# The first chunk's loads and masks put back, and the last store of the last chunk halved, in an mLSTM cell with a GELU feed-forward block

## The chip, the cores and the metric

The kernel runs on one core of a Trainium2 chip. The core has a matrix engine (TensorE, PE in the profile; PEld is its loading of weights), VectorE (DVE), ScalarE (ACT), GpSimd (POOL), and SyncE (SP), which here only issues transfers (DMA). The engines run beside each other, each through its own instructions in order, and wait for each other by semaphores. The metric is the time of one execution on the device, in microseconds.

## The reference

There are 4 batches of 8 heads, a sequence of 768 steps and a head size of 40. An mLSTM cell runs over the sequence, and its output goes through two matrix products with a GELU between them:

```python
for t in range(S):
    m_new = np.maximum(f_gate[:, :, t] + m, i_gate[:, :, t])
    f_stab = np.exp(f_gate[:, :, t] + m - m_new)
    i_stab = np.exp(i_gate[:, :, t] - m_new)
    m = m_new
    C = f_stab[..., None, None] * C + i_stab[..., None, None] * np.einsum('bhd,bhe->bhde', vt, kt)
    n = f_stab[..., None] * n + i_stab[..., None] * kt
    h_tilde = np.einsum('bhde,bhe->bhd', C, qt)
    denom = np.maximum(np.abs(np.einsum('bhd,bhd->bh', n, qt)[:, :, None]), 1.0)
    y[:, :, t] = sigmoid(o_gate[:, :, t]) * h_tilde / denom
x = y.transpose(0, 2, 1, 3).reshape(B * S, H * D)     # 3072 x 320
h = x @ w_in                                          # 320 x 2048
out = (h * sigmoid(1.702 * h)) @ w_out                # 2048 x 320
```

## The kernel before

The sequence is cut into six chunks of 128 steps. In a chunk the recurrence is written as a masked product: scores (queries times keys) are multiplied by weights exp(...) that come from running sums and maxima of the gates, and the product is multiplied by the values. The first chunk has no earlier state. Its weights are built on TensorE from the gates, split in three bf16 parts (`m3`, `a3`). The loads of the first chunk, the conversion of the feed-forward weights and the first chunk's attention all happen at the start; from the second chunk on, a chunk's attention runs beside the feed-forward products of the chunk before.

The parts that the change touches, with cuts marked:

```python
def load_gates(w):
    for dst, src in ((f_sb, f_gate), (i_sb, i_gate)):
        dst[w] = ld.tile([BH, L], FP, tag="fi", bufs=4, name="fi")
        (nc.sync if w > 1 else nc.scalar).dma_start(
            out=dst[w], in_=src[:, :, w * L:(w + 1) * L].rearrange("b h s -> (b h) s"))
# ... cut ...
load_gates(0)
load_gates(1)
for what, n in (("kq", 0), ("kq", 1), ("vo", 0), ("vo", 1), ("kq", 2), (fetch, 0), ("kq", 3),
                (fetch, 1), ("vo", 2), ("vo", 3), *((fetch, n) for n in range(2, 10))):
    ...        # "kq", n: keys and queries of batch n; "vo": values and output gate; fetch: a weight piece
# ... cut ...
keep_busy(7, ps_m, "m")                # filler products on TensorE
# ... cut ...
def clear(t):
    A.copy(out=t, in_=idle[:, 0:1].to_broadcast(t.shape))
# ... cut ...
def gates(w):                          # running sum and maximum on VectorE
    V.tensor_tensor_scan(out=f_run, data0=ones, data1=f_sb[w], ...)            # L258
    V.tensor_tensor(out=a, in0=i_sb[w], in1=f_run, op=OP.subtract)             # L260
    if w == 0:
        V.tensor_tensor(out=neg, in0=f_run, in1=i_sb[w], op=OP.subtract)
        in_three(G, a3, neg, neg, part)                                        # GpSimd
    V.tensor_tensor_scan(out=m_run, data0=ones, data1=a, initial=m, ...)       # L266
    if w == 0:
        in_three(V, m3, m_run, left, part)                                     # VectorE
    ...
# ... cut ...
def causal(x, n):
    G.affine_select(out=x, in_=x, compare_op=OP.is_ge, fill=0.0, base=0, pattern=[[0, n], [1, L]],
                    channel_multiplier=-1)                                     # L325

def weights(w, b):
    if w == 0:
        for i in range(2):
            pw = ps_a.tile([L, NP, L], FP, tag="a", name="p_w")
            if b > 1:                                                          # mask as a product, L334
                T.matmul(pw, ident_bf, not_yet.unsqueeze(1).to_broadcast([L, NP, L]), start=True, stop=False)
            for p in range(NP):
                T.matmul(pw[:, p, :], one, m3, start=(b < 2), stop=False)
                T.matmul(pw[:, p, :], a3, one, start=False, stop=(b < 2 or p == NP - 1))
            A.activation(out=x[:, :, i, :], in_=pw, func=AF.Exp)               # L340
            if b < 2:
                causal(x[:, :, i, :], NP)
        return
    ...
def scores(w, b):
    ...                                                                        # TensorE, L361
    for i in range(2):
        V.tensor_tensor(out=wt[w, b][:, :, i, :], in0=pw[i], in1=wt[w, b][:, :, i, :], op=OP.mult)   # L363
# ... cut: the order of the first chunk ...
transposes(0, 0)
transposes(0, 1, slice(0, 1))          # keys of batch 1
weights(0, 0)
transposes(0, 1, slice(1, 2))          # queries of batch 1
gates(1)
scores(0, 0)
weights(0, 1)
scores(0, 1)
gate_out(0)
gate_out(1)
clear(k_bl.rearrange("p j g c -> p (j g c)"))
values(0, 0)                           # TensorE, L373
values(0, 1)
transposes(0, 2)
convert(0, "A")                        # a weight piece: the part on ScalarE ("A"), on VectorE ("V")
weights(0, 2)
# ... cut ...
clear(state.rearrange("p j a b -> p (j a b)"))
# ... cut ...
convert(2, "V", slice(0, 256))
convert(3)
convert(4)
convert(2, "V", slice(256, 512))
```

At the other end, the second feed-forward product of a chunk is made in seven half-sized products for each pair of batches. Each goes by an addition on VectorE (L631) into the halves of two output tiles, which are then stored:

```python
def store(two):
    b = 2 * c + two
    nc.sync.dma_start(out=out[b * S + w * L:b * S + (w + 1) * L, :], in_=o[two])

return [lambda: product(block(0, 0), w00, (o00, None), (o01, None)),
        lambda: product(block(0, 1), w10, (o00, o00)),          # o00 is final here
        lambda: product(summed(1), t2, (o01, o01)),
        lambda: product(block(1, 0), w01, (o10, o01)),
        lambda: product(summed(0), t1, (o11, o10), (o01, o01)),
        lambda: (product(block(1, 1), t4, (o10, o10)), store(1)),
        lambda: (product(summed(2), w11, (o01, o01)), store(0))]
```

Of the kernel before, what the change touches and what calls it, by code (L numbers as in the profile page):

```python
# [12 lines left out]
OP = mybir.AluOpType  # L13
# [9 lines left out]
L = 128  # L23
# [11 lines left out]
def kernel(  # L35
# [12 lines left out]
    nc = tc.nc  # L48
    B, H, S, D = q.shape
    BH = B * H  # L50
    DM = H * D
    DFF = moe_w_in.shape[1]
    NW = S // L
    NP = H // 2
# [5 lines left out]
    DH = DM // 2  # L60
# [10 lines left out]
    ps_m = ctx.enter_context(tc.tile_pool(name="ps_m", bufs=2, space=PSUM))  # L71
# [3 lines left out]
    V, A, G, T = nc.vector, nc.scalar, nc.gpsimd, nc.tensor  # L75
# [6 lines left out]
    q_bl, k_bl = (const.tile([128, BH // 2, L // 32, 32], FP, name=name) for name in ("q_bl", "k_bl"))  # L82
# [11 lines left out]
    def load_gates(w):  # L94
        for dst, src in ((f_sb, f_gate), (i_sb, i_gate)):
            dst[w] = ld.tile([BH, L], FP, tag="fi", bufs=4, name="fi")
            (nc.sync if w > 1 else nc.scalar).dma_start(
                out=dst[w], in_=src[:, :, w * L:(w + 1) * L].rearrange("b h s -> (b h) s"))

    def load(w, what, bs=slice(0, B)):  # L100
        hs = slice(bs.start * H, bs.stop * H)
# [48 lines left out]
    pieces = []  # L150
# [4 lines left out]
    bits = {}  # L155
# [12 lines left out]


    load_gates(0)  # L170
    load_gates(1)
    for what, n in (("kq", 0), ("kq", 1), ("vo", 0), ("vo", 1), ("kq", 2), (fetch, 0), ("kq", 3),
                    (fetch, 1), ("vo", 2), ("vo", 3), *((fetch, n) for n in range(2, 10))):
        if isinstance(what, str):
            load(0, what, slice(n, n + 1))
        else:
            what(n)
# [5 lines left out]
    not_yet, ident_bf = (xs.bitcast(BF)[:, i * L:(i + 1) * L] for i in range(2))  # L183
# [3 lines left out]
    def keep_busy(n, pool=ps_a, tag="a"):  # L187
        p_idle = pool.tile([128, W], FP, tag=tag, name="p_idle")
        for _ in range(n):
            T.matmul(p_idle, idle, idle.unsqueeze(1).to_broadcast([128, 4, 128]), start=True, stop=True)  # L190

    keep_busy(7, ps_m, "m")
    ident = const.tile([128, 128], FP, name="ident")
    make_identity(nc, ident)
    one1 = const.tile([BH, 1], FP, name="one1")
# [9 lines left out]
    for t in (k_st, q_st):  # L205
# [3 lines left out]
                    channel_multiplier=-1)  # L209
    V.tensor_copy(out=ident_bf, in_=ident)  # L210

    a3 = const.tile([3 * BH, L], BF, name="a3")
    m3 = const.tile([3 * BH, L], BF, name="m3")
    state = const.tile([128, BH // 2, 2, D1], FP, name="state")

    def clear(t):
        A.copy(out=t, in_=idle[:, 0:1].to_broadcast(t.shape))


    t1, t2, t4 = (const.tile([128, NH, DH], FP, name=f"t{i}") for i in (1, 2, 4))  # L220

# [1 line left out]
    cols, stacked, m_row, dec = {}, {}, {}, {}  # L223
    kT, qT, wt, ys, xT, gs, o_ps, p_c = {}, {}, {}, {}, {}, {}, {}, {}


    def convert(n, engines="AV", part=slice(0, 512)):

        lo, hi, dst = bits[n][:, part, 0], bits[n][:, part, 1], pieces[n][0][:, part]
        dst_u = dst.bitcast(U32)  # L230
        if "A" in engines:
            A.activation(out=dst, in_=hi.bitcast(FP), func=AF.Abs)
            A.activation(out=lo, in_=lo, func=AF.Copy, scale=2.0 ** -29)
        if "V" not in engines:
            return
        V.tensor_scalar(out=dst, in0=dst, scalar1=HI_MIN, scalar2=HI_MAX, op0=OP.max, op1=OP.min)
        V.tensor_scalar(out=dst_u, in0=dst_u, scalar1=3, scalar2=0x3FFFFFFF, op0=OP.logical_shift_left,
                        op1=OP.bitwise_and)
        V.scalar_tensor_tensor(out=dst_u, in0=hi, scalar=0xC0000000, in1=dst_u, op0=OP.bitwise_and,
                               op1=OP.bitwise_or)  # L240
        V.tensor_tensor(out=dst_u, in0=dst_u, in1=lo, op=OP.add)
# [59 lines left out]
    def transposes(w, b, which=slice(0, 2)):  # L301
        for bl, st, dst, name in ((k_bl, k_st, kT, "kT"), (q_bl, q_st, qT, "qT"))[which]:
            dst[w, b] = work.tile([128, NP, L], FP, tag=name, bufs=4, name=name)
            if w:
                V.transpose(out=dst[w, b].rearrange("p j t -> p (j t)"),
                            in_=bl[:, b * NP:(b + 1) * NP].rearrange("p j g c -> p (j g c)"))
                continue
            pt = ps_a.tile([128, NP, L], FP, tag="a", name="p_t")
            for p in range(NP):
                h = b * H + 2 * p  # L310
                T.transpose(pt[:, p, :], st[:, h:h + 2, :].rearrange("p a b -> p (a b)"), ident)
            if b == 0:
                keep_busy(1)
            A.copy(out=dst[w, b], in_=pt)
# [5 lines left out]
            nc.sync.dma_start(out=x.rearrange("s p i t -> s (p i) t"),  # L320
                              in_=m_row[w][b * H:(b + 1) * H, :].unsqueeze(0).to_broadcast([L, H, L]))

    def causal(x, n):

        G.affine_select(out=x, in_=x, compare_op=OP.is_ge, fill=0.0, base=0, pattern=[[0, n], [1, L]],  # L325
                        channel_multiplier=-1)

    def weights(w, b):
        if w == 0:
            x = wt[w, b] = work.tile([L, NP, 2, L], FP, tag="wt", bufs=4, name="wt")  # L330
            for i in range(2):
                pw = ps_a.tile([L, NP, L], FP, tag="a", name="p_w")
                if b > 1:
                    T.matmul(pw, ident_bf, not_yet.unsqueeze(1).to_broadcast([L, NP, L]), start=True, stop=False)  # L334
                for p in range(NP):
                    h = b * H + 2 * p + i
                    one = pick[:, h:h + 1].to_broadcast([3 * BH, L])
                    T.matmul(pw[:, p, :], one, m3, start=(b < 2), stop=False)
                    T.matmul(pw[:, p, :], a3, one, start=False, stop=(b < 2 or p == NP - 1))
                A.activation(out=x[:, :, i, :], in_=pw, func=AF.Exp)  # L340
                if b < 2:
                    causal(x[:, :, i, :], NP)
            return
        x = wt[w, b].rearrange("s p i t -> s (p i) t")
        for h in range(H):
            A.activation(out=x[:, h, :], in_=x[:, h, :], func=AF.Exp, scale=-1.0,  # L346
                         bias=cols[w][:, b * H + h:b * H + h + 1])
        causal(x, H)
        if w > 1 and b == 0:
            gates_out(w)  # L350

    def gates_out(w):
        A.activation(out=eo[w], in_=eo[w], func=AF.Tanh, scale=0.5)
# [238 lines left out]
    w10, w11 = w_out_sb[:, NH:NF, 0:DH], w_out_sb[:, NH:NF, DH:DM]  # L592
# [16 lines left out]
    def total(i, c):  # L609

        return (xs if i == 0 and c else big[:, i, :]).rearrange("p (f t) -> p f t", t=L)

    def down_fast(w, c):
        o = [op.tile([128, DM], FP, tag="o", name="o_sb") for _ in range(2)]
        o00, o01, o10, o11 = (o[i][:, n * DH:(n + 1) * DH] for i in range(2) for n in range(2))

        def block(two, k):
            return lambda f: gs[w, k * 4 + f // 2][:, f % 2, (2 * c + two) * L:(2 * c + two + 1) * L]

        def summed(i):  # L620
            return lambda f: total(i, c)[:, f, :]

        def product(a, b, *adds):
            po = ps_m.tile([128, DH], FP, tag="m", name="p_out")
            for f in range(NH):
                T.matmul(po, a(f), b[:, f, :], start=(f == 0), stop=(f == NH - 1))  # L626
            for dst, x in adds:
                if x is None:
                    V.tensor_copy(out=dst, in_=po)
                else:  # L630
                    V.tensor_tensor(out=dst, in0=x, in1=po, op=OP.add)  # L631

        def store(two):
            b = 2 * c + two
            nc.sync.dma_start(out=out[b * S + w * L:b * S + (w + 1) * L, :], in_=o[two])

        return [lambda: product(block(0, 0), w00, (o00, None), (o01, None)),
                lambda: product(block(0, 1), w10, (o00, o00)),
                lambda: product(summed(1), t2, (o01, o01)),
                lambda: product(block(1, 0), w01, (o10, o01)),  # L640
                lambda: product(summed(0), t1, (o11, o10), (o01, o01)),
                lambda: (product(block(1, 1), t4, (o10, o10)), store(1)),
                lambda: (product(summed(2), w11, (o01, o01)), store(0))]

# [24 lines left out]
    def gate_out(b):  # L671
        z = eo[0][:, b * H:(b + 1) * H, :]
        A.activation(out=z, in_=z, func=AF.Tanh, scale=0.5)
# [11 lines left out]
    V.tensor_reduce(out=pair, in_=ident[0:BH, 0:BH].rearrange("p (j two) -> p j two", two=2), axis=AX.X, op=OP.add)  # L685
    V.tensor_copy(out=half[0:BH], in_=par.unsqueeze(2).to_broadcast([BH, 2, 64]))
    transposes(0, 0)
    transposes(0, 1, slice(0, 1))
    weights(0, 0)
    transposes(0, 1, slice(1, 2))  # L690
    gates(1)
    scores(0, 0)
    weights(0, 1)
    scores(0, 1)
    gate_out(0)
    gate_out(1)
    clear(k_bl.rearrange("p j g c -> p (j g c)"))
    values(0, 0)
    values(0, 1)
    transposes(0, 2)  # L700
# [11 lines left out]
    columns(0)  # L712
    gate_out(2)
    gate_out(3)
    clear(state.rearrange("p j a b -> p (j a b)"))
    scale(0, 0)
    scale(0, 1)

# [16 lines left out]
    full_rows(0, 1, 0)  # L735
    seam(0, 3)
    full_rows(1, 1, 0)

    convert(2, "V", slice(0, 256))
    convert(3)  # L740
    convert(4)
    convert(2, "V", slice(256, 512))
    for j in range(2):
        for c in range(2):
            full_rows(j, c, 1)
# [132 lines left out]
```

## Time and profile before

| what | value |
|---|---|
| time, median of 3 runs | 489.21 us (487.54 to 490.1) |
| span of the profiled execution | 485.8 us |
| instructions | 10430 |
| DMA moved | 44.87 MB, 175953 packets, mean 92 GB/s |

The page gives each engine's busy time and its share of the span, then the span in 40 slices of about 12.1 us, one digit for each (tenths, 9 is 90% or more), for the engines and for the DMA engines. A line of an answer on the timeline has the start and duration in us, the engine, the line of the kernel, the operation, what it writes and reads with its shape, and in brackets how long the engine stood idle before it and what ended that. An answer on waits has the total, the number of times and the longest, in us. A group in the timeline can hold several instructions (x16): its duration is from the first start to the last end.

### The profile page before, as it was taken

How to read it: one execution, taken by the hardware profiler on the slowest of the kernel's cores; microseconds unless marked ns; L12 is line 12 of the kernel's file. 1: busy time of each engine (PE TensorE's matmuls, PEld its weight loads, DVE VectorE, ACT ScalarE, POOL GpSimd, SP SyncE). 2: the span in 40 equal slices, each digit the busy share in tenths (PEclk: the TensorE clock that was granted, in tenths of full speed). 3: DMA queues.
4: the chain of work that ended last, by engine and by line, in shares of the span. 5: the costliest groups of instructions: out<-in, count | busy, mean ns of one | idle time of the engine just before them, and what ended most of it. 6: DMA issues, size and time to landing. Idle time of an engine off the chain costs nothing. (4 is left out here: it accounts for less than half of the span.)

```text
span 485.8 us, 10430 instructions
## 1 busy us (share of the span) xinstructions
PE 477.8 (98%) x4067; PEld 396.8 (82%) x4067; DVE 343.7 (71%) x857; ACT 220.2 (45%) x575; POOL 62.6 (13%) x105
## 2 busy tenths in 40 slices
PE   8899999999999999999999999999999999999997
PEld 5784457777879999788999877999977999977997
DVE  7889879787978965667766686696576786254831
ACT  3776768203559401467700465900374920255300
POOL 4120003420000430000331000232000120000000
PEclk9999999999999999999999999999999999999999
DMA  9999789823996100997000796300393000000000
GB/s 135 207 274 325 164 154 245 91 41 69 154 214 69 19 28 29 164 201 80 7 29 2 120 252 74 32 28 3 78 258 29 2 15 16 28 1 0 1 27 28
DMA packets 175953, 44.87 MB, mean 92 GB/s; under 512 B 164352, under 2 KB 169504, under 8 KB 175904
## 3 DMA queue, kind: packets, MB, share of 16 engines
q1 hardware_dynamic: 175136, 43.48, 48.6%
q8 instruction: 32, 0.52, 0.5%
q10 hardware_dynamic: 768, 0.72, 0.4%
q14 instruction: 17, 0.14, 0.1%
HBM read 40.17 MB, written 4.01 MB: 91 GB/s over the span
## 5 line engine op out<-in xcount | busy, mean ns | idle before, releaser
L626 PE MATMUL p_out<-w_out_sb,g 128*128 128x160 f32 x480 | 69.8, 301 | 0.0
L416 ACT COPY xT<-p_x 128x384 f32<-128x384 f32 x24 | 10.8, 482 | 127.5 <-PE p_x L415 114.4
L626 PEld LDWEIGHTS p_out<-w_out_sb,g 128*128 128x128 f32 x480 | 66.3, 190 | 0.9
L537 DVE TENSOR_TENSOR g<-p_u,g 128x256 f32<-128x256 f32 x80 | 33.7, 424 | 44.6 <-PE p_u L529 35.0
L534 ACT COPY g<-p_u 128x256 f32<-128x256 f32 x120 | 43.0, 377 | 43.5 <-PE p_u L529 39.3
L541 ACT ACTIVATE g<-g 128x256 f32<-128x256 f32 x120 | 42.3, 423 | 39.4 <-DVE g L537 39.4
L325 POOL TENSOR_SCALAR_AFFINE_SELECT wt<-wt 128x1024 f32<-128x1024 f32 (+1 forms) x24 | 25.2, 1054 | 236.3 <-ACT wt L346 187.1
L631 DVE TENSOR_TENSOR o_sb<-o_sb,p_out 128x160 f32<-128x160 f32 x70 | 21.4, 317 | 42.2 <-PE p_out L626 41.8
L346 ACT ACTIVATE wt<-wt,cols 128x128 f32<-128x128 f32 x160 | 47.9, 394 | 0.0
L529 PE MATMUL p_u<-xT,w_in_sb 128*128 128x256 f32 x160 | 38.9, 382 | 0.0
L529 PE MATMUL p_u<-xs,big 128*128 128x256 f32 x160 | 37.9, 379 | 0.0
L557 PE MATMUL p_u<-xT,w_in_x 64*128 64x512 f32 x80 | 37.0, 602 | 0.0
L557 PE MATMUL p_v<-xT,w_in_x 64*128 64x512 f32 x80 | 37.0, 602 | 0.0
L577 PE MATMUL p_out<-w_out_sb,g 128*128 128x320 f32 x128 | 36.3, 436 | 0.0
L363 DVE TENSOR_TENSOR wt<-p_s,wt 128x512 f32<-128x512 f32 x48 | 30.4, 682 | 8.1 <-POOL wt L325 6.7
L626 PE MATMUL p_out<-t,big 128*128 128x160 f32 x240 | 35.5, 301 | 0.0
L529 PEld LDWEIGHTS p_u<-xT,w_in_sb 128*128 128x128 f32 x160 | 29.6, 190 | 5.4 <-DVE o_sb L631 1.5
L529 PEld LDWEIGHTS p_u<-xs,big 128*128 128x128 f32 x160 | 30.0, 190 | 4.6
L626 PEld LDWEIGHTS p_out<-t,big 128*128 128x128 f32 x240 | 33.3, 190 | 0.2
L577 PEld LDWEIGHTS p_out<-w_out_sb,g 128*128 128x128 f32 x128 | 23.8, 190 | 9.8 <-issue 0.5
L537 DVE TENSOR_TENSOR g<-p_v,g 128x256 f32<-128x256 f32 x80 | 29.8, 414 | 0.0
L361 PE MATMUL p_s<-qT,kT 40*128 40x128 f32 x384 | 25.7, 280 | 1.9 <-DVE wt L363 1.6
(172 smaller groups left out, 844.8 us busy)
## 6 DMA issues: line engine op xcount, KB each, us to landing
wt<-m_row SPq DMA_DIRECT2D x20, 512.0 KB, 6.6
v_st<-in_v_dram SPq DMA_DIRECT2D x5, 640.0 KB, 9.0
eo<-in_o_gate_dram SPq DMA_DIRECT2D x5, 640.0 KB, 6.0
k_st<-in_k_dram SPq DMA_DIRECT2D x5, 640.0 KB, 11.0
out_dram<-o_sb SPq DMA_DIRECT2D x20, 160.0 KB, 1.8
big<-in_moe_w_in_dram SPq DMA_DIRECT2D x5, 512.0 KB, 7.4
k_bl<-in_k_dram SPq DMA_DIRECT2D x40, 64.0 KB, 2.9
q_bl<-in_q_dram SPq DMA_DIRECT2D x40, 64.0 KB, 2.8
```

Of the source, the lines that this page charges most:

```text
L325: G.affine_select(out=x, in_=x, compare_op=OP.is_ge, fill=0.0, base=0, pattern=[[0, n], [1, L]], channel_multiplier=-1)
L346: A.activation(out=x[:, h, :], in_=x[:, h, :], func=AF.Exp, scale=-1.0, bias=cols[w][:, b * H + h:b * H + h + 1])
L361: T.matmul(pw[i][:, p, :], kT[w, b][r, p, :], qT[w, b][r, p, :], start=True, stop=True)
L363: V.tensor_tensor(out=wt[w, b][:, :, i, :], in0=pw[i], in1=wt[w, b][:, :, i, :], op=OP.mult)
L529: T.matmul(p[k][:, ts[t]], a[:, k // 2, k % 2 * 128:(k % 2 + 1) * 128], b, start=first, stop=True, skip_group_check=True)
L534: A.copy(out=g[k][i][:, ts[t]], in_=chain[k][:, ts[0]])
L537: V.tensor_tensor(out=g[k][i][:, ts[t]], in0=p[k][:, ts[pt]], in1=g[k][i][:, ts[t]], op=OP.add)
L541: A.activation(out=dst, in_=dst if src is None else src, func=AF.Gelu_apprx_sigmoid)
L557: T.matmul(p[k], w_in_x[r, k, :], x[r, 2, :], start=False, stop=True, skip_group_check=True)
L577: T.matmul(po, gs[w, f // 2][:, f % 2, b * L:(b + 1) * L], w_out_sb[:, f, :], start=(f == 0), stop=(f == NF - 1))
L626: T.matmul(po, a(f), b[:, f, :], start=(f == 0), stop=(f == NH - 1))
L631: V.tensor_tensor(out=dst, in0=x, in1=po, op=OP.add)
```

## The change

The change takes back a set of edits to the first chunk, and adds one edit to the last chunk. In the first chunk all gate loads are issued by SyncE again, those of the second chunk behind the keys and queries of batches 0 and 1; the causal mask of batches 0 and 1 is again a product on TensorE and not a select on GpSimd; the keys of batch 1 are transposed with its queries; the two clears stand at the top of ScalarE's program; piece 2 is converted in one go; and there is one more filler product. In the last chunk the left half of batch 2's output rows, which is final after the second product of seven, is stored at once, so that the last store of the kernel has 160 columns and not 320.

```diff
-            (nc.sync if w > 1 else nc.scalar).dma_start(
-                out=dst[w], in_=src[:, :, w * L:(w + 1) * L].rearrange("b h s -> (b h) s"))
+            nc.sync.dma_start(out=dst[w], in_=src[:, :, w * L:(w + 1) * L].rearrange("b h s -> (b h) s"))
 load_gates(0)
-load_gates(1)
-for what, n in (("kq", 0), ("kq", 1), ("vo", 0), ...
+for what, n in (("kq", 0), ("kq", 1), (load_gates, 1), ("vo", 0), ...
-    keep_busy(7, ps_m, "m")
+    keep_busy(8, ps_m, "m")
-    def clear(t):
+    for t in (k_bl.rearrange("p j g c -> p (j g c)"), state.rearrange("p j a b -> p (j a b)")):
         A.copy(out=t, in_=idle[:, 0:1].to_broadcast(t.shape))
# ... cut: weights(0, b) ...
-                if b > 1:
-                    T.matmul(pw, ident_bf, not_yet..., start=True, stop=False)
+                T.matmul(pw, ident_bf, not_yet..., start=True, stop=False)
-                    T.matmul(pw[:, p, :], one, m3, start=(b < 2), stop=False)
-                    T.matmul(pw[:, p, :], a3, one, start=False, stop=(b < 2 or p == NP - 1))
+                    T.matmul(pw[:, p, :], one, m3, start=False, stop=False)
+                    T.matmul(pw[:, p, :], a3, one, start=False, stop=(p == NP - 1))
-                if b < 2:
-                    causal(x[:, :, i, :], NP)
# ... cut: down_fast ...
+        last = w == NW - 1 and c == 1
-        def store(two):
+        def store(two, cols=slice(0, DM)):
             b = 2 * c + two
-            nc.sync.dma_start(out=out[b * S + w * L:b * S + (w + 1) * L, :], in_=o[two])
+            nc.sync.dma_start(out=out[b * S + w * L:b * S + (w + 1) * L, cols], in_=o[two][:, cols])
+        def left_done():
+            if last:
+                store(0, slice(0, DH))
-                lambda: product(block(0, 1), w10, (o00, o00)),
+                lambda: (product(block(0, 1), w10, (o00, o00)), left_done()),
-                lambda: (product(summed(2), w11, (o01, o01)), store(0))]
+                lambda: (product(summed(2), w11, (o01, o01)), store(0, slice(DH if last else 0, DM)))]
# ... cut: the order of the first chunk ...
-    transposes(0, 1, slice(0, 1))
     weights(0, 0)
-    transposes(0, 1, slice(1, 2))
+    transposes(0, 1)
-    clear(k_bl.rearrange("p j g c -> p (j g c)"))
-    clear(state.rearrange("p j a b -> p (j a b)"))
-    convert(2, "V", slice(0, 256))
+    convert(2, "V")
     convert(3)
     convert(4)
-    convert(2, "V", slice(256, 512))
```

More of the change, by code (lines that the diff above doesn't have):

```diff
@@ L170 @@
     load_gates(0)
-    load_gates(1)
-    for what, n in (("kq", 0), ("kq", 1), ("vo", 0), ("vo", 1), ("kq", 2), (fetch, 0), ("kq", 3),
+    for what, n in (("kq", 0), ("kq", 1), (load_gates, 1), ("vo", 0), ("vo", 1), ("kq", 2), (fetch, 0), ("kq", 3),
                     (fetch, 1), ("vo", 2), ("vo", 3), *((fetch, n) for n in range(2, 10))):
@@ L224, with convert @@
     kT, qT, wt, ys, xT, gs, o_ps, p_c = {}, {}, {}, {}, {}, {}, {}, {}
-    def convert(n, engines="AV", part=slice(0, 512)):
-        lo, hi, dst = bits[n][:, part, 0], bits[n][:, part, 1], pieces[n][0][:, part]
+    def convert(n, engines="AV"):
+        lo, hi, dst = bits[n][:, :, 0], bits[n][:, :, 1], pieces[n][0]
         dst_u = dst.bitcast(U32)
@@ L321, in spread @@
                               in_=m_row[w][b * H:(b + 1) * H, :].unsqueeze(0).to_broadcast([L, H, L]))
-    def causal(x, n):
-        G.affine_select(out=x, in_=x, compare_op=OP.is_ge, fill=0.0, base=0, pattern=[[0, n], [1, L]],
-                        channel_multiplier=-1)
     def weights(w, b):
@@ L332, in weights @@
                 pw = ps_a.tile([L, NP, L], FP, tag="a", name="p_w")
-                if b > 1:
-                    T.matmul(pw, ident_bf, not_yet.unsqueeze(1).to_broadcast([L, NP, L]), start=True, stop=False)
+                T.matmul(pw, ident_bf, not_yet.unsqueeze(1).to_broadcast([L, NP, L]), start=True, stop=False)
                 for p in range(NP):
@@ L347, in weights @@
                          bias=cols[w][:, b * H + h:b * H + h + 1])
-        causal(x, H)
+        G.affine_select(out=x, in_=x, compare_op=OP.is_ge, fill=0.0, base=0, pattern=[[0, H], [1, L]],
+                        channel_multiplier=-1)
         if w > 1 and b == 0:
```

## The prediction

> **What bounds the kernel now.** I read the page first: the busy shares, the 40 slices and the chain that ended last. Then I asked for TensorE's waits over the whole span, because the page shows it as the only nearly full engine, and then for the timeline of the first 31 us and of the last 10 us, which are the two places that the change touches. Last came the landings of the first loads, one by one.
>
> ```profile
> span 485.8 us, 10430 instructions
> ...
> PE 477.8 (98%) x4067; PEld 396.8 (82%) x4067; DVE 343.7 (71%) x857; ACT 220.2 (45%) x575; POOL 62.6 (13%) x105
> ...
> PE   8899999999999999999999999999999999999997
> ...
> DMA  9999789823996100997000796300393000000000
> ```
>
> TensorE (PE) is busy for 477.8 of 485.8 us. All that the two ends of the kernel can give or take is within the 8.0 us left: the first two slices (8, 8) and the last (7). Everything between is TensorE in its own order. The DMA row says that the first 75 us or so are also full of transfers, so a load that starts later is a suspect there. TensorE's waits, over the whole span:
>
> ```profile
> PE p_s L361 <- DVE wt L363: 1.6, 1, 1.6
> PE p_idle L190 <- DVE idle L184: 1.1, 1, 1.1
> PE p_w L338 <- DVE m L251: 0.9, 1, 0.9
> PE p_out L626 <- DVE o_sb L631: 0.4, 1, 0.4
> PE p_s L361 <- ACT wt L340: 0.4, 1, 0.4
> PE p_t L311 <- DMA k_st<-in_k_dram: 0.3, 1, 0.3
> ```
>
> Six waits of 0.3 us or more in the whole kernel (one of 0.2 is left out), all but one before 21 us, so the start must be read as a chain. The lines of the timeline that carry it (start, duration, engine; in brackets the idle time before it and what ended it):
>
> ```profile
> 3.58 0.41 DVE L258 TENSOR_TENSOR_SCAN f_run<-one,fi 32x128 f32<-32x128 f32 x1
> 5.67 0.28 DVE L260 TENSOR_TENSOR st<-fi,f_run 32x128 f32<-32x128 f32 x1 [1.68 <-DMA fi<-in_i_gate_dram]
> 8.60 0.23 PE L338 MATMUL p_w<-m,pick 96*128 96x128 bf16 x1 [0.86 <-DVE m L251]
> 9.91 0.41 DVE L258 TENSOR_TENSOR_SCAN f_run<-one,fi 32x128 f32<-32x128 f32 x1
> 10.20 1.27 POOL L325 TENSOR_SCALAR_AFFINE_SELECT wt<-wt 128x512 f32<-128x512 f32 x2 [1.40 <-ACT wt L340]
> 10.35 0.62 DVE L260 TENSOR_TENSOR st<-fi,f_run 32x128 f32<-32x128 f32 x1
> 12.70 0.62 DVE L285 TENSOR_SCALAR dec_in<-pair,both 32x16 f32<-32x16 f32 x1
> 13.24 1.27 DVE L363 TENSOR_TENSOR wt<-p_s,wt 128x512 f32<-128x512 f32 x2
> 13.97 1.16 PE L361 MATMUL p_s<-qT,kT 40*128 40x128 f32 x16 [1.56 <-DVE wt L363]
> 15.23 1.29 DVE L363 TENSOR_TENSOR wt<-p_s,wt 128x512 f32<-128x512 f32 x2 [0.72 <-PE p_s L361]
> 16.57 1.02 PE L373 MATMUL p_o<-v_st,wt 128*64 128x41 f32 x28 [0.24 <-DVE wt L363]
> ```
>
> The reader is to see one chain: the input gate lands (5.67), the first chunk's gates are computed and split in three (to 8.6), the first weights follow (exponential, mask on POOL to 11.47), and then VectorE, which computes the second chunk's gates from 9.91 on, comes to its first product of scores and weights only at 13.24, although the scores were finished at 11.41 (the L361 group of 10.25, 1.16 us). TensorE waits 1.56 us for that product. From 16.57 on it has one wait of 0.36 us left until the end of the first part, so whatever the start gains or loses by 16.57 should stand at the end of the kernel.
>
> At the other end the last addition and the last two stores:
>
> ```profile
> 481.04 2.51 SPq L635 DMA_DIRECT2D out_dram<-o_sb  x2
> 482.86 0.32 DVE L631 TENSOR_TENSOR o_sb<-o_sb,p_out 128x160 f32<-128x160 f32 x1 [1.85 <-PE p_out L626]
> ```
>
> The addition ends at 483.18, the last store is issued then and lands 1.8 us after its issue (about 485.0), and the span closes at 485.8.
>
> [...] the first input-gate load, 16 KB issued by ScalarE at 1.29, took 4.3 us to land, between key loads of 160 KB that took 3.4 to 5.0. The second issuer did not make it a fast load.
>
> [...] L260, two SBUF inputs, takes 0.28 us at 5.67, and 0.62 at 10.35 under POOL's select of 10.20 to 11.47; the scan L266 takes 0.47 alone and 0.73 there; L285 takes 0.62 under the second pair of selects.
>
> [...] This trace has 1.8 us for the whole store of 160 KB[...]; the 16 KB stores of m_row took 1.4 us in the median, which gives (1.8 - 1.4) x 80/144 = 0.22 us for halving the size.
>
> **The change part by part.**
>
> 1. Two gate loads move ahead of the first keys on SyncE's queue. An issue of a gate load there takes 0.42 us (median of the later ones), with the gap about 0.48; two of them put the first keys' issue from 0.81 to about 1.8, so everything behind them lands about 1.0 us later: first keys 4.2 to 5.2, first queries 5.5 to 6.5, second keys 6.9 to 7.9, second queries 7.9 to 8.9. The first gates gain: with nothing ahead of it but the forget gate, the input gate should land after about 2.7 us, as the first forget gate did (0.80, needed at 3.58), so at about 4.1 instead of 5.6. The scans then run 1.5 us earlier: the split in three ends on VectorE at about 7.0 and on POOL at 7.2, instead of 8.55 and 8.81.
>
> 2. The first weights then wait for TensorE's own order, not for the gates: first-query transposes from 6.5, some 0.9 us at the still slow rate, and the filler after them to about 7.7. Start of the weights: 7.7 against 8.60, a gain of 0.9.
>
> 3. Mask on TensorE in place of POOL for batches 0 and 1. Added: four matmuls L334 of 0.38 us. In the third batch, which has them already, matmuls begin 0.22 us after the mask's, so I count 0.22 x 2 = 0.44 us for a batch. Removed: the POOL selects, four of 0.65 us (two in 1.27), of which the end past the exponentials counts: 11.47 - 10.56 = 0.91 us. So batch 0's weights are complete at 7.7 + 1.5 (two groups of 0.75) + 0.7 (the last exponential) = 9.9, instead of 11.47.
>
> 4. Second keys' transposes go behind the weights. That adds 0.63 us of TensorE ahead of the first scores. Both second transposes then run 9.2 to 10.4, and the scores 10.4 to 11.55: the same time as before (11.41), within 0.2.
>
> 5. The second gates. Their loads are now issued seventh and eighth on SyncE's queue, at about 4.6 and 5.1, behind the second queries; small, they should land right behind them, at 9.0 to 9.5 (before: 5.9 and 6.65). VectorE reaches them at about 8.3, and waits. Its work there took 13.24 - 9.91 = 3.33 us before; without POOL beside it (0.62 to 0.28, 0.73 to 0.47, 0.62 to about 0.17) it is 1.05 less, so 2.3 us: 9.2 + 2.3 = 11.5. The first product thus starts at about 11.6 and not at 13.24: 1.6 us earlier.
>
> 6. From there batch 1: weights with masks on TensorE 11.55 to 13.05, scores to 14.2, product at 14.25 against 15.23. TensorE's second half of the values starts about 15.6 against 16.57. Gain carried into the dense part: about 1.0 us.
>
> 7. The clears (1.90 and 1.28 us on ScalarE, at 13.69 and 27.24) move to the first 5.5 us, where ScalarE does nothing until the first keys' copy at about 6.3: no cost, and no gain on TensorE, which didn't wait for ScalarE there.
>
> 8. The second half of weight piece 2's conversion is put ahead of pieces 3 and 4: 0.78 us more (half of 0.43+0.43+0.69+0.69, less overlaps, from L236 to L241 at 30.57 to 32.2). VectorE stood idle 0.87 us just before piece 3 (L236 at 33.07), which takes it up: 0. One more filler matmul, 0.43 us, lies in the wait for the first keys: 0.
>
> 9. The last store is half as large, and the left half is stored some 10 us earlier, beside TensorE's work: -0.2 us. VectorE's later additions go to the other half, and I see no wait of theirs on that store.
>
> Sum: -1.0 (start) - 0.2 (end) = -1.2 us at face value.
>
> **The rivals.** First, the loads' delay comes through. Everything on SyncE's queue is about 1.0 us later, and if the second gates land later than 9.5 (the backlog ahead of them is 640 KB), each us of that is a us of the first product: at 11 they would land for a product at 13.3 and the start would gain nothing. For it: in later chunks gate loads behind a backlog took up to 11.4 us. Against: only four loads are ahead of them. The time would be 489.
>
> Second, later loads take the place of the removed waits. Piece 1 lands at 20.1 and ScalarE takes it at 22.01; both move towards each other by 1.0 us, and 0.1 is missing. The last output gate lands at 24.6, needed 27.0; piece 2 lands at 26.9, taken at 28.42 behind a clear of 1.28 that goes away. These have slack of nil to 1 us. If they bind, the start loses some of its gain but hardly goes below nothing: 488.5 to 489.5.
>
> Third, the parts removed were worth what they were made for: first keys 1.0 us earlier, and second keys transposed in a hole of TensorE. Then the kernel is 1 us slower in the start and 0.2 faster at the end: 490. For it: TensorE's first transposes did wait for keys, and there will be some 0.5 us more of that. The clock adds a doubt: [...] The trace agrees with a switch (the filler L190 took 0.63 us early, 0.38 at 6.48), and a hole of 0.5 us between 4.7 and 5.2 may put it off.
>
> **Range and chances.** I weigh my own chain at a little over half, and the two rivals that eat it at the rest: 0.55 x (-1.2) + 0.3 x (-0.2) + 0.15 x (+0.8) = -0.6, so 489.2 - 0.6 = 488.6 us. Three runs of the kernel before span 2.6 us by themselves (487.54 to 490.1); with 1 us of doubt on the change, a range of 486.8 to 490.4. Two per cent are 9.8 us, more than all of TensorE's idle time (8.0), so faster by that much can't follow from these parts; slower by it would need a jam of the loads that I don't see: 0.01 and 0.02.
>
> **What would show it.** Right: the first VectorE product of scores and weights near 11.6, the second half of batch 1's values on TensorE near 15.6, VectorE's second L260-like subtraction near 0.28 us, first keys' transposes near 5.2, no POOL select before 20 us, TensorE without new waits from 20 to 75 us, and a last store of about 1.6 us. Wrong: a wait of VectorE for the second gates' loads past 10; TensorE idle for a DMA or for a converted piece between 20 and 45 us; or a later addition waiting for the early store.

## The result, and the profile after

The changed kernel takes 485.88 us in the median of 6 runs (485.65 to 486.87). The kernel before, run beside it, takes 489.5 (487.54 to 490.88). The ratio is 0.993, with a 95% interval of 0.9907 to 0.9952. I had forecast 488.6 and a range of 486.8 to 490.4: the time lies outside that range, and the gain of 3.6 us is six times the forecast 0.6.

The page of the changed kernel (PEclk is the clock that TensorE was granted, in tenths of its full speed):

```profile
span 485.1 us, 10434 instructions
...
PE 479.3 (99%) x4072; PEld 397.8 (82%) x4072; DVE 343.0 (71%) x853; ACT 220.6 (45%) x575; POOL 60.4 (12%) x101
...
PE   8999999999999999999999999999999999999997
...
PEclk9999999999999999999999999999999999999999
```

The span of this execution is 485.1 us, only 0.7 below the 485.8 of the one profiled before. That is the first thing to notice: the two profiles differ by much less than the medians. The execution profiled before (487.54) was the fastest of its six, the one profiled after (486.87) the slowest. TensorE's waits:

```profile
PE p_idle L188 <- DVE idle L182: 1.1, 1, 1.1
PE p_out L615 <- DVE o_sb L620: 0.4, 1, 0.4
PE p_o L362 <- DVE wt L352: 0.4, 1, 0.4
PE p_s L350 <- ACT wt L330: 0.4, 1, 0.4
PE p_t L307 <- DMA k_st<-in_k_dram: 0.3, 1, 0.3
```

The wait of 1.6 us for VectorE's first product and the 0.9 for the first gates are gone. The start, in the lines of the timeline that answer to those of before (scan, subtraction, weights, second gates, products):

```profile
3.85 0.28 DVE L256 TENSOR_TENSOR st<-fi,f_run 32x128 f32<-32x128 f32 x1
4.99 1.09 PE L307 MATMUL p_t<-ident,k_st 128*128 128x128 f32 x4 [0.34 <-DMA k_st<-in_k_dram]
7.27 0.38 PE L324 MATMUL p_w<-xs 128*128 128x512 bf16 x1
8.64 0.41 DVE L254 TENSOR_TENSOR_SCAN f_run<-one,fi 32x128 f32<-32x128 f32 x1 [0.49 <-DMA fi<-in_f_gate_dram]
9.09 0.28 DVE L256 TENSOR_TENSOR st<-fi,f_run 32x128 f32<-32x128 f32 x1
10.84 0.22 DVE L281 TENSOR_SCALAR dec_in<-pair,both 32x16 f32<-32x16 f32 x1
10.98 1.27 DVE L352 TENSOR_TENSOR wt<-p_s,wt 128x512 f32<-128x512 f32 x2
12.11 1.35 PE L350 MATMUL p_s<-qT,kT 40*128 40x128 f32 x16
13.37 1.29 DVE L352 TENSOR_TENSOR wt<-p_s,wt 128x512 f32<-128x512 f32 x2 [1.12 <-PE p_s L350]
14.71 0.90 PEld L362 LDWEIGHTS p_o<-v_st,wt 128*64 128x64 f32 x28 [0.19 <-DVE wt L352]
```

The input gate no longer holds the first subtraction (3.85, before 5.67). The first product starts at 10.98 (before 13.24), the second at 13.37 (before 15.23), and the second scores follow without a wait. TensorE's second half of the values, at 16.57 before, comes 1.86 us sooner, at 14.71.

### The profile page after: what moved, and what is told of

The parts are those of the page before. It is cut to its first block, busy times and chain, and to the rows that moved or that the text cites. A ratio compares the mean times of both kernels' runs of the same rounds, so it can differ in the third digit from the quotient of the medians.

```text
span 485.1 us, 10434 instructions
## 1 busy us (share of the span) xinstructions
PE 479.3 (99%) x4072; PEld 397.8 (82%) x4072; DVE 343.0 (71%) x853; ACT 220.6 (45%) x575; POOL 60.4 (12%) x101
## 5 line engine op out<-in xcount | busy, mean ns | idle before, releaser
L336 POOL TENSOR_SCALAR_AFFINE_SELECT wt<-wt 128x1024 f32<-128x1024 f32 x20 | 22.7, 1136 | 240.9 <-ACT wt L334 201.9
L546 PEld LDWEIGHTS p_v<-xT,w_in_x 64*128 64x128 f32 x80 | 14.2, 186 | 16.0 <-issue 16.0
```

Source lines behind the costliest of these rows:

```text
L546: T.matmul(p[k], w_in_x[r, k, :], x[r, 2, :], start=False, stop=True, skip_group_check=True)
```

## The experiments

Each of the kernels was run on the chip beside the kernel before. "b" names start from the kernel before, "a" names from the changed one.

**The two halves of the change.** `last_only` is the kernel before with the early half store alone; `first_only` is the changed kernel without it:

```diff
-        last = w == NW - 1 and c == 1
+        last = False
```

> The first chunk's edits as in the change, the last store of the kernel whole as before. Theory A (the start's chain is 1.86 us shorter, the rest of the 3.6 us comes with it): 486.2, that is all but 0.2 to 0.4 us of the gain. Rival B (the early half store at the end frees something larger): 487.5 to 488.5.

> The kernel before, with only the last store halved. Theory A: 489.5 - 0.2 to 0.4 = 489.2, not told apart from before. Rival B: 487 to 488.

`first_only`: 485.84 us (6 runs, 485.77 to 486.29), ratio 0.9921 (0.9899 to 0.9943). `last_only`: 488.98, ratio 0.9994 (0.9978 to 1.001). So the gain is in the first chunk's edits, and nothing of it can be measured at the end. Rival B falls.

**The kernel before once more**, for a second profile, because the first one didn't fit its own median.

> The kernel before, unchanged, for a second profile. Theory A with a lottery in the loads (the profiled execution of before, 487.54, was the fastest of its six): the time is about 489.5 and the profile shows TensorE waiting 1 to 2 us for attention of the second chunk at 80 to 86 us, where loads arrive later than in the first profile. Rival: the span is the same everywhere and the 2 us lie elsewhere (start, end, or a slower clock).

489.18 us (22 runs, 486.78 to 490.98). I had the place wrong, and the rival in its last words ("a slower clock") was right: the profiled execution shows no loss at 80 to 86 us, but a slow clock. The row on the granted clock in its page:

```profile
PEclk9799999999999999999999999999999999999999
```

and in its answer on stretches (the stretch and its length; busy time and number of instructions for PE, PEld, DVE, ACT and POOL; the granted clock, the DMA share, GB/s):

```profile
10.00:15.00 5.00, 3.44 (x66) 3.03 (x64) 4.13 (x10) 4.02 (x6) 2.10 (x4) 1.00 1.21 202
15.00:20.00 5.00, 5.00 (x65) 4.44 (x62) 3.59 (x12) 0.94 (x2) 0.47 (x2) 0.53 1.10 211
20.00:25.00 5.00, 5.00 (x49) 4.39 (x47) 3.20 (x6) 4.63 (x10) 0.00 (x0) 0.79 0.87 182
```

The same stretches of the first profile of before:

```profile
10.00:15.00 5.00, 3.44 (x51) 2.92 (x49) 4.33 (x10) 4.03 (x8) 2.49 (x4) 1.00 1.21 202
15.00:20.00 5.00, 4.76 (x96) 4.29 (x93) 3.99 (x13) 2.37 (x5) 0.47 (x2) 1.00 1.07 211
20.00:25.00 5.00, 4.63 (x50) 3.74 (x49) 4.54 (x9) 4.90 (x11) 0.00 (x0) 1.00 0.93 191
```

The stretch from 10 to 15 us, with the hole in TensorE (the time in which it idles), is the same in both (3.44 us busy). Behind it the second profile runs at half clock from 15.3 to 22.1 us (the granted clock is 1.00 from 14.90 to 15.20, 0.50 from 15.30 to 15.60 and from 21.80 to 22.00, and 1.00 from 22.10 to 22.40): in the stretch from 15 to 20 TensorE is busy all the time and gets 65 instructions done instead of 96. Aligned matmul by matmul, this execution is 0.6 us ahead of the first profile at 15 us and 1.4 us behind it at 23, a loss of 2.0 us. The profile of `last_only` has the same, from 13.2 to 20.1 us (0.50 from 13.30 to 13.60 and from 19.80 to 20.00). This became theory K: the hole at the start costs, besides its own length, a stretch at half clock in most executions.

**Fillers in the holes.** A test of K that shortens no chain:

```diff
     transposes(0, 1, slice(0, 1))
+    keep_busy(2, ps_x, "x")
     weights(0, 0)
 # ... cut ...
     weights(0, 1)
+    keep_busy(5, ps_x, "x")
     scores(0, 1)
```

> The kernel before, with seven filler products on TensorE in its two holes: two ahead of the first weights, five ahead of the second scores. They compute nothing that is used, and nothing waits less: the first product of scores and weights stays at 13.0 to 13.3. Theory K ([...] which costs 1.7 to 2 us in most executions of before, and none in the first profile): clock 1.0 in the profile, 487.4 to 487.9, with a spread of about 1 us. Rival (only the chain counts): 489.2 or more, since it is not shortened.

`b_fill_second` has the five in the second hole alone: does that hole bring the slow clock, or do both together?

> The kernel before, with only the five filler products ahead of the second scores, where TensorE waits 1.6 us for VectorE. [...] as with both fillers, 487.2 with a spread of 1 us. If the two holes together do: part of the executions keep a low clock, the median is 487.5 to 488.5 and the spread 2 us or more.

The clock on record for an execution is the mean over its span: 6.8 us at half clock in 487 us, as in the profiles of `before_again` and `last_only`, give about 0.993 (on record 0.992 and 0.993), and 3.4 us, as in the profile of `a_mask_pool` below, give about 0.996 (on record 0.996).

`b_filler`: 487.2 us (22 runs, 486.91 to 488.12), before beside it 488.67 (42 runs, 486.81 to 491.59), ratio 0.9975 (0.9963 to 0.9987). The line in its timeline where the first product starts:

```profile
12.65 1.27 DVE L363 TENSOR_TENSOR wt<-p_s,wt 128x512 f32<-128x512 f32 x2
```

That is the start in the second profile of before, to the digit, so the chain is untouched; seven products that compute nothing make the kernel 1.5 us faster in the median, and take away the slow tail (its slowest is below the median of before), while the fastest stays where it was (486.91, 486.81 before). The clock of the stretch behind the hole:

```profile
15.00:20.00 5.00, 4.76 (x86) 4.13 (x82) 4.18 (x14) 2.37 (x6) 0.47 (x2) 1.00 1.11 213
```

The single executions say the same. All 22 of `b_filler` have a clock of 0.999 or 1.0. Of the kernel before there are 148 executions with a clock on record: the 34 at 0.999 or more take 487.2 us in the median, as `b_filler` does, and the 114 below take 489.4. With the five fillers in the second hole alone: 487.13, ratio 0.9967 (0.9954 to 0.998), but 2 of 17 executions are at 490.2, and these two have a clock of 0.993. The second hole is most of it.

**The hole put into the changed kernel.** The opposite test: two writes of zeros on VectorE ahead of its first product.

```diff
     gates(1)
+    V.memset(t1.rearrange("p n m -> p (n m)"), 0.0)
+    V.memset(t2[:, 0:4, :], 0.0)
     scores(0, 0)
```

> The changed kernel, with two writes of zeros (1920 columns, about 1.6 us, into tiles that are filled anew later) on VectorE ahead of its first product, so that the first product starts at about 12.6 and TensorE gets a hole of about 1.5 us as before. Chain alone: 485.9 + 1.6 = 487.5 with a spread of 1 us. With theory K (the hole costs clock in part of the executions): median 488 to 489, spread 3 us, and a low clock in the records of those above 488.5.

489.16 us (22 runs, 487.64 to 491.16): ratio to before 1.0009 (0.9996 to 1.0022), that is all of the gain gone. The first product and the clock behind it:

```profile
13.07 1.21 DVE L352 TENSOR_TENSOR wt<-p_s,wt 128x512 f32<-128x512 f32 x2
13.74 1.97 PE L350 MATMUL p_s<-qT,kT 40*128 40x128 f32 x16 [1.93 <-DVE wt L352]
```

```profile
10.00:15.00 5.00, 2.97 (x39) 2.24 (x36) 3.92 (x9) 1.92 (x5) 0.00 (x0) 1.00 1.26 195
15.00:20.00 5.00, 5.00 (x76) 4.70 (x73) 3.27 (x11) 0.00 (x0) 0.24 (x1) 0.51 1.12 217
```

The product is 2.1 us later than in the changed kernel (13.07 - 10.98), but the changed kernel's TensorE had no wait there, so it is TensorE's second scores that count: they start 1.6 us later (13.74 - 12.11), which alone makes 485.9 + 1.6 = 487.5, as expected for the chain alone. The rest, 1.6 us, is K's. The single executions bear this out: the only one with a clock of 1.0 takes 487.64, and the other 21, with 0.99 to 0.996, take 488.83 or more.

**The parts of the first chunk's edits, one at a time.**

```diff
 # b_gates_sp: the loads alone
-            (nc.sync if w > 1 else nc.scalar).dma_start(
+            nc.sync.dma_start(
-    load_gates(1)          # and (load_gates, 1) behind ("kq", 1)
 # b_mask_pe: the masks alone
-                if b > 1:
-                    T.matmul(pw, ident_bf, not_yet..., start=True, stop=False)
+                T.matmul(pw, ident_bf, not_yet..., start=True, stop=False)
-                if b < 2:
-                    causal(x[:, :, i, :], NP)
```

> The kernel before, with only the gate loads as after the change: all by SyncE, those of the second chunk behind the keys and queries of two batches. Chain: the input gate lands 1.5 us earlier, the first product starts at about 11.7 (13.24 before), GpSimd's masks still beside the second gates. If the loads' order is the main part: 486.2 to 487, with clock 1.0. If the mask is: 488 to 489.

> The kernel before, with only the masks of batches 0 and 1 as products on TensorE. Chain: the second gates take 2.3 us on VectorE instead of 3.3, the first product starts at about 12.2. By the chain alone 488.2; if the shorter hole also keeps the clock, 486.5 to 487.5.

> The changed kernel with the masks of batches 0 and 1 as selects on GpSimd, as before the change. The first product comes later, by the end of the selects (0.9 us past the exponentials) and by the second gates' slower work beside them: 11.6 to 12.0 instead of 10.98. 486.2 to 486.9, with clock 1.0 as in the run with only the gate loads.

| kernel | median us (runs, range) | ratio to before, 95% | first product |
|---|---|---|---|
| `b_gates_sp` | 486.18 (7, 485.93 to 486.57) | 0.9941 (0.9919 to 0.9963) | 11.65 |
| `b_mask_pe` | 486.86 (10, 486.27 to 487.31) | 0.9954 (0.9935 to 0.9972) | 11.42 |
| `a_mask_pool` | 485.78 (6, 485.69 to 487.01) | 0.9936 (0.9923 to 0.995) | 11.73 |

The loads' order alone brings nearly all of it. The masks alone bring most of it as well (I had put the first product at 12.2, read from the first profile; here the input gate landed 0.8 us sooner, at 4.76), but on top of the loads they bring nothing that can be measured: with the masks on GpSimd the changed kernel is as fast (and I had expected 0.3 to 1.0 us more). Both edits do the same thing, bringing the first product to about 11.5, and TensorE's wait for it from 1.6 to 0.8 us or less, so their gains don't add. The changed kernel with the masks on GpSimd still waits 1.1 us, and one of its six executions, the one profiled, has a clock of 0.996.

**Moving the second gates.** Both kernels, with VectorE's second gates behind the products of batches 0 and 1:

```diff
-    gates(1)
     scores(0, 0)
     weights(0, 1)
     scores(0, 1)
+    gates(1)
```

> The kernel before, with the second chunk's gates on VectorE put behind the two products of scores and weights of batches 0 and 1. If VectorE's work on the second gates (3.3 us beside GpSimd) is what held the first product at 13.24: that product starts at about 11.5 and the time falls by 1 to 1.8 us, to about 488. If the mask on GpSimd or the late input gate holds it as well: less than 0.5 us.

> The changed kernel, with the second chunk's gates on VectorE behind the products of batches 0 and 1. The first product is then held by the scores alone (finished at 10.74, product at 10.98 now): 0.2 us less at the start, 485.6. If the work moved back then holds up the values' normalisation at 14.6: 486 or more.

`b_gates_late`: 487.3 us (9 runs), ratio 0.9949 (0.9926 to 0.9971). The first product starts at 11.41, so the second gates were what held it; but against the first profile TensorE's lead of 1.4 us at 15 us shrinks to 0.4 by 21, where it waits for the first chunk's output: the work was moved, not saved. What is left of the gain is about what the fillers give, and 8 of the 9 executions have a clock of 0.999 or 1.0. `a_gates_late`: 486.99 (16 runs, 486.56 to 489.66), 1.1 us slower than the changed kernel; the last part of my expectation was the right one. Fifteen of the 16 have a clock of 0.999 or 1.0, so most of this spread has another cause than the clock; none was looked for.

**Second gates' loads on ScalarE, in the changed kernel**, an attempt to beat it.

```diff
-            nc.sync.dma_start(out=dst[w], ...)
+            (nc.scalar if w == 1 else nc.sync).dma_start(out=dst[w], ...)
+    load_gates(1)          # at the start; (load_gates, 1) behind ("kq", 1) goes
```

> The changed kernel, with the second chunk's gate loads issued by ScalarE at its start, those of the first chunk by SyncE. The second gates land by about 6.5 (8.6 now), so VectorE starts them at 8.15 and not at 8.64; the first product is then held by the scores (10.74): 0.2 us at the start. The values, output gates and later loads are issued about 1.0 us earlier, which may spare some of the 0.4 to 1.1 us that TensorE loses at 83 us to late loads. 485.3 to 485.9[...].

486.26 us (6 runs, 485.53 to 486.95), not told apart from the changed kernel and above the 485.3 to 485.9 that I expected. The first product starts at 10.58, 0.4 us sooner, but TensorE now has a wait of 1.5 us for ScalarE at 23 us, which stands behind the conversion of a weight piece whose load lands later (21.9 us after the start, 20.6 in the changed kernel). None of the kernels tried beats the changed one by more than the ranges allow.

## Why the prediction was wrong

**The chain at the start was right in kind and too small.** Input gate, key issue, weights, second gates, first product came in the predicted order:

| step | before | predicted | measured |
|---|---|---|---|
| issue of the first keys | 0.81 | 1.8 | 1.72 |
| first weights on TensorE | 8.60 | 7.7 | 7.27 |
| second gates start on VectorE | 9.91 | 9.2 | 8.64 |
| their length | 3.33 | 2.3 | 2.34 |
| first product | 13.24 | 11.6 | 10.98 |
| second product | 15.23 | 14.25 | 13.37 |

The length without GpSimd beside it came out to a few hundredths (L256 at 9.09 takes 0.28 us, where L260 took 0.62). The landings were the mis-sized term of this chain. I put every load 1.0 us later; the first keys were issued 0.9 later and landed 0.6 later, and the second queries landed only 0.4 later (all from the trace). So the first rival (late second gates) did not happen: VectorE waited 0.49 us for them. The lead at the second half of the values was 1.86 us, not 1.0.

**Part of that lead is an accident of the first profile.** The start of the kernel before hangs on the landing of the input gate. In the first profile it lands at 5.58 us and the first product starts at 13.24; in `before_again` at 5.00 and 12.65, in `last_only` at 4.85 and 12.51, each time 7.7 us later. The first profile has the latest landing of the seven that keep this order of loads (4.76 to 5.58; 2.90 to 3.06 in those with the changed order). Against `before_again` TensorE's second half of the values comes 1.27 us sooner (15.98 to 14.71), not 1.86.

**Some of it is lost again**, as the second rival had it, though mostly at other places than it named. In the profile of `first_only` the lead over the first profile of before falls from 1.66 us to 1.44 near 24 us and to 1.25 near 126; I haven't tested either. In the profiled execution of the changed kernel it falls at 83 us:

```profile
78.74 0.68 ACT L228 ACTIVATE w_out_sb<-big 128x512 f32<-128x512 f32 x1 [4.88 <-DMA big<-in_moe_w_out_dram]
83.36 2.21 PE L362 MATMUL p_o<-v_st,wt 128*64 128x41 f32 x60 [0.37 <-DVE wt L352]
```

A weight piece whose last part `first_only` has at 75.5 us lands at 78.6 here, ScalarE waits 4.9 us for it, VectorE's product and then TensorE's values come late, and the lead goes down from 1.72 to 0.71. The other five executions of the changed kernel have spans of 483.9 to 484.2 us against the 485.1 of this one, so this loss belongs to the one execution and not to the change. It is why the two profiles lie only 0.7 us apart.

**The step that failed is the term "-1.0 (start)" of the sum, and the sentence that it rests on: "whatever the start gains or loses by 16.57 should stand at the end of the kernel".** It priced the removed hole of 1.56 us at its length. The runs showed that in most executions of the kernel before the hole also costs clock: TensorE runs at half clock behind it, for 6.8 us in the profile of `before_again`, which loses 2.0 us there, nearly all of it after that point. No term stood for that. The half clock isn't in the first profile at all (clock 1.0 throughout), and in none of the six executions of the changed kernel (clock 1.0 in each). In the medians the sum is: 489.2 to 487.2 for keeping the clock (the fillers; 1.2 to 2.0 us, depending on whether the ratio or this difference is taken), and 487.2 to 485.85 for the shorter chain (1.35 us).

That the 1.2 us at face value come near these 1.35 is luck: the chain's lead was put 0.86 too low, the profile that it was read against starts 0.6 late, and the store gave 0.07 instead of 0.2. The forecast of 0.6 then gave half of the 1.2 up to rivals of which only the second came, and that in part (0.1 to 0.4 us).

**The range hid the same thing.** "Three runs of the kernel before span 2.6 us by themselves": I took that spread as noise of the measurement and subtracted a chain read from one profile from the median of three. But the profile belonged to the execution at 487.54, 1.7 us below that median, and the question why was not asked.

I had raised the clock for a hole of 0.5 us that the change makes, and not for the hole of 1.56 us that it takes away. In the profiles the half clock lasts about 6.8 us in `before_again`, `last_only` and `a_hole` (there the granted clock is 0.51 in the stretch from 15 to 20 and 0.80 in that from 20 to 25), and 3.4 in `a_mask_pool` (granted clock 1.00 from 13.40 to 13.60, 0.50 from 13.70 to 14.00 and from 16.80 to 17.00, 1.00 from 17.10 to 17.40), where a wait of 1.1 us is left. In `before_again` it begins at 15.3 us, when TensorE has been busy again for 1.9 us (since 13.38).

Why the first profile escaped was not shown. The length of the hole alone does not sort the profiles: the first one of before has a hole of 1.56 us (12.41 to 13.97), as `before_again` has (11.82 to 13.38), and a clock of 1.0 throughout; `b_gates_late` has a wait of 1.0 us and a clock of 1.0, `a_mask_pool` one of 1.1 us and a half clock. No run here moved a hole and left its length.

**The third rival did not happen**: later first keys cost TensorE 0.34 us of waiting at 4.99, which the gates' lead covers. The filler that takes 0.38 us where the earlier ones take 0.63 starts at 7.06 us, 6.48 before.

**The last store.** Predicted -0.2. It landed 1.6 us after its issue instead of 1.8, but the span closed 2.57 us after the last addition in the changed kernel and 2.64 before, so 0.07 us reached the end, below what `last_only` could show.

**No cost was seen**, as predicted, of the clears, the filler, and the order of piece 2. They weren't run alone, so none of them is measured.

## What to carry to other kernels

When the profiled execution is faster than the median, or runs of one kernel spread more than those of its neighbours, profile it again before taking a chain from it: what costs the time may not be in the first profile. The hole of 1.56 us in a nearly full TensorE cost more than its length here (1.2 to 2.0 us came back in the median with fillers that shorten no chain), so look at the granted clock behind each hole, and at the clock of every execution beside its time; fillers that compute nothing are the cheap test. Gate loads of 16 KB ahead of the 160 KB loads cost the large ones about half a microsecond in the changed kernel (landings 0.4 to 0.6 us later), and brought the first product forward by 1.0 to 1.6 us (`b_gates_sp` against the two profiles of before).

## What was not expected of the hardware

The half clock began only at the end of the hole (`last_only`: TensorE idle from 12.9 to 13.2 us at a clock of 1.00, full from 13.3 at 0.50) or after it, when TensorE was full again (`before_again`: work again from 13.38, half clock from 15.3), and in the profiles lasted 3.4 us (`a_mask_pool`) or about 6.8 (`before_again`, `last_only`, `a_hole`); in the stretch from 15 to 20 us of the second profile of before, 65 matmuls were done instead of 96. And a spread of 4.2 us over 22 executions of one kernel (486.78 to 490.98) shrank to 1.2 us (486.91 to 488.12) by seven matmuls on zeros.
